# Loading the first tile in halves and reordering the first microseconds of a tuned state-space and dense block

## The chip, the cores and the metric

The kernel runs on one core of one Trainium2 chip. The metric is the device time of one execution in microseconds (us). The kernel before takes 624.6 us (median of three runs, 624.42 to 625.04). All runs quoted here are at a granted TensorE clock of 1.00 or 0.999. The profile's span is about 2 us shorter than the time.

The engines are TensorE (PE; its weight loads are PEld), VectorE (DVE), ScalarE (ACT), GpSimd (POOL) and SyncE (SP, which here only issues DMAs). A letter q after an engine's name, as in SPq, is its sequencer issuing a DMA.

## The reference

The input x is [2048, 1024]. It is normalised row by row; the result goes through a diagonal complex recurrence with two projections (branch A) and through a dense layer with the Mish function (branch B), and both are added to x.

```
xn  = (x - mean) / sqrt(var + 1e-5)                  # per row
A   = 2 * Re(C @ h),  h[t] = Lam_bar * h[t-1] + B_bar @ xn[t],   plus xn * Dskip
B   = act(xn @ w1 + b1) @ w2,   act(h) = h * tanh(softplus(h))
out = x + A + B
```

## The kernel before

The 2048 rows are worked in four blocks of 512 rows, each of four tiles of 128 rows. In each block TensorE does the first dense layer (28 column groups f, 8 matmuls each), the input projection of the recurrence, and then the second dense layer and the output projection. Everything before the first real matmul of block 0 is the head: the rows must be loaded, normalised and transposed. That is what the change is about.

Each buffer has a record of its last writer and readers, and a helper turns it into semaphore waits; so the order of the calls below is the order on each engine. `vop`, `aop` and `pop` queue an operation on VectorE, ScalarE and GpSimd.

```
    for q in range(NQ):                      # four tiles of x, 256 KB each, on SyncE's queue
        load_x(SP, 0, q)
    ...                                      # then w1 (seven ring slots of 512 KB) on the same queue

    keep_busy(76)                            # 76 filler matmuls before the transposes
    ...
    for q in range(2):                       # tiles 0 and 1: sums on VectorE
        first_sums_v(q, 0)
        first_sums_v(q, 1)
        first_var_v(q)
    first_sqrt(0)
    first_mean_a(2)                          # tile 2: sums on ScalarE
    first_sqrt(1)
    first_var_a(2)
    first_sqrt(2)
    first_apply(0)                           # xn of tile 0, VectorE
    first_transpose(0)                       # 8 transposes on TensorE into PSUM
    keep_busy(4)
    first_apply(1)
    first_transpose(1)
    keep_busy(4)
    first_copy(0, VE)                        # PSUM to SBUF
    first_copy(1, VE, 0, 4)
    first_copy(1, AC, 4, NK)
    first_mean_a(3)                          # tile 3: sums on ScalarE
    first_var_a(3)
    first_sqrt(3)
    first_apply(2)
    first_apply(3)
    NSPLIT = 6
    # [...]
    for f in range(NSPLIT):
        first_half(f, 0)                     # 8 matmuls of 256 columns: tiles 0 and 1 only
        if f == 0:
            ...                              # transpose of the parameters, copy to par
        if f in (2, 3):
            q = f
            first_transpose(q)               # tiles 2 and 3 join here
            first_copy(q, VE)
```

After f=5 the second halves of f=0 to 5 (tiles 2 and 3) follow, and from f=6 on matmuls have all 512 columns. So f=6 is where the head's effect ends for TensorE.

GpSimd works through a chain of phases that starts when VectorE has computed `thp`, which it does in program order right after the copy of tile 3:

```
    def phases(j):                           # eight times, all on GpSimd
        xs, b_xs = ph_slot(j)
        pop(... px = iot * thp[j] ...)
        pop(... py = round(px) ...)
        pop(... xs = px - py ...)
```

VectorE in block 0 evicts the dense layer's results (`hb`), multiplies the Mish results (`act<-act,hb`, "mish products"), computes statistics for block 1, and multiplies the projection by tables (`mt<-ps,tab`, two operations for each of eight j). TensorE needs the PSUM banks of the last of those products before it can go on with the second dense layer.

Of the kernel before, what the change touches and what calls it, by code (L numbers as in the profile page):

```python
# [5 lines left out]
ALU = mybir.AluOpType  # L6
# [3 lines left out]
P = 128  # L10
# [146 lines left out]
def build_kernel(nc, A_x, A_Lambda_re, A_Lambda_im, A_B_re, A_B_im, A_C_re, A_C_im,  # L157
                 A_log_dt, A_Dskip, B_w1, B_b1, B_w2, out):
    bf16, f32, i32 = DT.bfloat16, DT.float32, DT.int32
    S, D = A_x.shape[1], A_x.shape[2]  # L160
# [4 lines left out]
    NQ = TB // P  # L165
    NK = D // P
# [8 lines left out]
    PE = Queue(nc, "pe")  # L175
    VE = Queue(nc, "ve")
    AC = Queue(nc, "ac")
    PO = Queue(nc, "po")
    SP = Queue(nc, "sp")

    def sb(name, shape, dtype):
        return nc.alloc_sbuf_tensor(name, shape, dtype)
# [4 lines left out]
    b_ring = [Buf("ring%d" % i) for i in range(NRING)]  # L187
# [16 lines left out]
    b_xnT = [Buf("xnT%d" % q, parts=[Buf("xnT%d_%d" % (q, h)) for h in range(2)]) for q in range(NQ)]  # L204
# [3 lines left out]
    xx = sb("xx", [P, 2, NQ, D], bf16)  # L208
    b_xx = [[Buf("xx%d_%d" % (i, q), parts=[Buf("xx%d_%d_%d" % (i, q, h)) for h in range(2)])
             for q in range(NQ)] for i in range(2)]  # L210
# [7 lines left out]
    NST = 3 * NJ + NF  # L218
    st = sb("st", [NST, P], bf16)
    b_st = Buf("st")  # L220
    ident = sb("ident", [P, P], bf16)
    b_ident = Buf("ident")
    par = sb("par", [P, NST], f32)
    b_par = Buf("par")
    stats = sb("stats", [P, 2, 2, 6], f32)
    b_stats = [Buf("stats%d" % i) for i in range(2)]
# [21 lines left out]
    ps = nc.alloc_psum_tensor("ps", [P, 8, TB], f32)  # L248
    b_ps = [Buf("ps%d" % i) for i in range(8)]

    def ps16(i):
        return ps[:, i, :].bitcast(bf16)
# [23 lines left out]
    vop, aop, pop = VE.op, AC.op, PO.op  # L276
# [7 lines left out]
    def load_x(queue, blk, q):  # L284
        r0 = blk * TB + q * P
        i = blk % 2
        queue.dma(lambda e: e.dma_start(xx[:, i, q, :], A_x[0, r0:r0 + P, :]),  # L287
                  s_xx[i][q] if blk else s_x0[q], writes=[b_xx[i][q]])

    for q in range(NQ):  # L290
        load_x(SP, 0, q)
    for src, r0, n in ((A_log_dt, 2 * NJ, NJ), (A_Lambda_im, NJ, NJ), (A_Lambda_re, 0, NJ),
                       (B_b1, 3 * NJ, NF)):
# [42 lines left out]
    def rc(q, n):  # L336
        return rs[:, q, n:n + 1]

    def first_sums_v(q, h):
        s = q % 2  # L340
        vop(lambda e: e.bn_stats(stats[:, s, h, :], xx[:, 0, q, h * 512:(h + 1) * 512]),
            reads=[b_xx[0][q]], writes=[b_stats[s]])

    def first_var_v(q):
        s = q % 2
        vop(lambda e: e.bn_aggr(mv[:, q, :], stats[:, s, :, :]), reads=[b_stats[s]], writes=[b_mv[q]])

    def first_mean_a(q):
        aop(lambda e: e.activation(sq[:], xx[:, 0, q, :], AF.Identity, bias=kon[:, 1:2], accum_out=rc(q, 3)),  # L349
            reads=[b_xx[0][q], b_kon], writes=[b_sq, b_rs[q]])  # L350
        aop(lambda e: e.activation(mv[:, q, 0:1], rc(q, 3), AF.Copy, scale=-1.0 / D),  # L351
            reads=[b_rs[q]], writes=[b_mv[q]])

    def first_var_a(q):
        aop(lambda e: e.activation(sq[:], xx[:, 0, q, :], AF.Square, bias=mv[:, q, 0:1], accum_out=mv[:, q, 1:2]),
            reads=[b_xx[0][q], b_mv[q]], writes=[b_sq, b_mv[q]])

    def first_sqrt(q):
        scale = 1.0 if q < 2 else 1.0 / D
        aop(lambda e: e.activation(rc(q, 1), mv[:, q, 1:2], AF.Sqrt, scale=scale, bias=kon[:, 2:3]),  # L360
            reads=[b_mv[q], b_kon], writes=[b_rs1[q]])

    def first_apply(q):
        y = rc(q, 1)
        vop(lambda e: e.reciprocal(y, y), reads=[b_rs1[q]], writes=[b_rs1[q]])  # L365
        vop(lambda e: e.tensor_scalar(xn[:, q, :], xx[:, 0, q, :], mv[:, q, 0:1], y,  # L366
                                      op0=ALU.subtract if q < 2 else ALU.add, op1=ALU.mult),
            reads=[b_xx[0][q], b_mv[q], b_rs1[q]], writes=[b_xn[q]])

    def bank_T(q, k):  # L370
        if q == 1 and k >= NK // 2:
            return 5
        return 6 + q % 2

    def first_transpose(q):
        for k in range(NK):
            bank = bank_T(q, k)
            PE.mm(lambda e, k=k, bank=bank: e.transpose(ps16(bank)[:, k * P:(k + 1) * P],  # L378
                                                        xn[:, q, k * P:(k + 1) * P], ident[:]),
                  reads=[b_xn[q], b_ident], writes=[b_ps[bank]],  # L380
                  first=k == 0 or bank != bank_T(q, k - 1), last=k == NK - 1 or bank != bank_T(q, k + 1))

    def first_copy(q, queue, k0=0, k1=NK):
        dst = xnT[:, k0:k1, q * P:(q + 1) * P]
        bank = bank_T(q, k0)
        srcp = ps16(bank).rearrange("p (k t) -> p k t", k=NK)[:, k0:k1, :]
        b_dst = b_xnT[q] if k1 - k0 == NK else b_xnT[q].parts[k0 // 4]
        if queue is AC:
            aop(lambda e: e.copy(dst, srcp), reads=[b_ps[bank]], writes=[b_dst])  # L389
        else:  # L390
            vop(lambda e: e.tensor_copy(dst, srcp), reads=[b_ps[bank]], writes=[b_dst])
# [62 lines left out]

    def keep_busy(n):
        for i in range(n):
            PE.mm(lambda e: e.matmul(ps[:, 4, 0:P], lhsT=ident[:], rhs=ident[:], start=True, stop=True),
                  reads=[b_ident], writes=[b_ps[4]], first=i == 0, last=i == n - 1)

    keep_busy(76)  # L460
    aop(lambda e: e.activation(rs[:, :, 3], kon[:, 2:3].to_broadcast([P, NQ]), AF.Sqrt), reads=[b_kon], writes=b_rs)
    for q in range(2):
        first_sums_v(q, 0)
        first_sums_v(q, 1)
        first_var_v(q)
    first_sqrt(0)
    first_mean_a(2)
    first_sqrt(1)
    first_var_a(2)
    first_sqrt(2)  # L470
    first_apply(0)
    first_transpose(0)
    keep_busy(4)
    first_apply(1)
    first_transpose(1)
    keep_busy(4)
    first_copy(0, VE)
    first_copy(1, VE, 0, 4)
    first_copy(1, AC, 4, NK)
    first_mean_a(3)  # L480
    first_var_a(3)
    first_sqrt(3)
    first_apply(2)
    first_apply(3)
    NSPLIT = 6

    def first_half(f, half):
        s, fi = f // 2, f % 2
        wt = ring[:, s, :].rearrange("p (k f) -> p k f", k=NK)
        ts = slice(half * 256, half * 256 + 256)  # L490
        for k in range(NK):
            PE.mm(lambda e, k=k: e.matmul(ps[:, f, ts], lhsT=wt[:, k, fi * P:(fi + 1) * P], rhs=xnT[:, k, ts],  # L492
                                          start=k == 0, stop=k == NK - 1),
                  reads=[b_ring[s]] + b_xnT[2 * half:2 * half + 2], writes=[b_ps[f]],
                  first=half == 0 and k == 0, last=half == 1 and k == NK - 1)

    for f in range(NSPLIT):
        first_half(f, 0)
        if f == 0:
            PE.op(lambda e: e.transpose(ps16(5)[:, 0:NST], st[:, :], ident[0:NST, 0:NST]),  # L500
                  reads=[b_st, b_ident], writes=[b_ps[5]])
            vop(lambda e: e.tensor_copy(par[:, :], ps16(5)[:, 0:NST]), reads=[b_ps[5]], writes=[b_par])
        if f in (2, 3):
            q = f
            first_transpose(q)
            first_copy(q, VE)

# [123 lines left out]
    def first_tile(blk, f):  # L631
        s = n_item[0] % NRING
        fi, bank, hs = f % 2, f % 8, f % (2 * GF)
        wt = ring[:, s, :].rearrange("p (k f) -> p k f", k=NK)
        if blk == 0 and f < NSPLIT:
            first_half(f, 1)
        for k in range(0 if blk == 0 and f < NSPLIT else NK):
            PE.mm(lambda e, k=k: e.matmul(ps[:, bank, :], lhsT=wt[:, k, fi * P:(fi + 1) * P], rhs=xnT[:, k, :],  # L638
                                          start=k == 0, stop=k == NK - 1),
                  reads=[b_ring[s]] + b_xnT, writes=[b_ps[bank]], first=k == 0, last=k == NK - 1)  # L640
        if fi == 1:
            item_done()
        if f % GF == 0 and f >= 2 * GF:
            mish_mul(f // GF - 2)
        vop(lambda e: e.tensor_scalar(hb[:, hs, :], ps[:, bank, :], b1(f), None, op0=ALU.add),  # L645
            reads=[b_ps[bank], b_par], writes=[b_hbf[hs]])
        if f % GF == GF - 1:
            mish(f // GF)
# [219 lines left out]
```

## Time and profile before

| quantity | value | where |
|---|---|---|
| time, median of 3 | 624.6 us | runs |
| span | 622.4 us | page |
| TensorE's share of the chain that ended last | 98% | page, part 4 |
| first real matmul | 9.78 us | timeline |
| first weight load of f=6 | 21.28 us | timeline |
| TensorE idle after 9.78 us, as the view counts it | 0.27 us, at 93 us | waits, timeline |

The first fence is the page, its lines for busy time and for the chain. The chain is followed back from the last instruction to what released each step.

```profile
PE 616.7 (99%) x2981; PEld 287.9 (46%) x2981; DVE 464.1 (75%) x684; ACT 246.7 (40%) x162; POOL 50.2 (8%) x47
...
PE 98%; DMA 1%; DVE 1%; ACT 0%; SPq 0%; issue 0%
```

TensorE is the bottleneck, and the rest of the chain is the head. The next fence is the timeline of the head (start, duration, engine, line, operation, output<-input, shapes, count; in brackets the idle time before it and what ended it).

```profile
0.79 1.84 SPq L287 DMA_DIRECT2D xx<-in_A_x_dram  x4
...
1.41 5.65 PE L457 MATMUL ps<-ident 128*128 128x128 bf16 x76 [1.41 <-POOL kon L328]
...
2.67 5.67 SPq L316 DMA_DIRECT2D ring<-in_B_w_dram  x4
...
3.57 1.42 DVE L341 BATCH_NORM_STATS2 stats<-xx 128x6 f32<-128x512 bf16 x2 [3.57 <-DMA xx<-in_A_x_dram]
...
5.90 1.15 ACT L349 ACTIVATE sq<-xx,kon 128x1024 bf16<-128x1024 bf16 x1 [0.34 <-DMA xx<-in_A_x_dram]
...
7.28 0.28 ACT L360 ACTIVATE rs<-mv,kon 128x1 f32<-128x1 f32 x1
7.43 0.62 PE L378 MATMUL ps<-ident,xn 128*128 128x128 bf16 x8 [0.36 <-DVE xn L366]
...
7.79 0.55 DVE L366 TENSOR_SCALAR xn<-xx,mv,rs 128x1024 bf16<-128x1024 bf16 x1
...
9.78 1.03 PE L492 MATMUL ps<-xnT,ring 128*128 128x256 bf16 x8 [0.54 <-ACT xnT L389]
```

The root of tile 1 (7.28) stands behind ScalarE's mean of tile 2 (5.90), and so tile 1 is normalised only at 7.79.

The chain in order of time, from the end of the head to block 1:

```profile
21.55 37.99 PE ps L638 x176
59.54 27.63 PE ps L658 x128
87.17 3.47 PE ps L715 x16
90.63 0.00 issue
90.64 2.37 DVE mt L663 x2
93.00 0.05 issue
93.05 70.54 PE ps L715 x326
163.58 6.47 PE ps L638 x30
```

At 90.64 the chain leaves TensorE for VectorE's last `mt` product and comes back at 93.05.

### The profile page before, as it was taken

Reading aid. Unit: us, or ns where it says so; the run is one execution under the profiler, and the core shown is the slowest. Engines: PE = TensorE matmul, PEld = TensorE weight load, DVE = VectorE, ACT = ScalarE, POOL = GpSimd, SP = SyncE. Lnnn points to the kernel's source line nnn. Section 1 sums busy time; section 2 is a strip of 40 time slices with the busy share of each in tenths; the row PEclk is TensorE's granted clock in tenths of the full one; section 3 lists DMA queues with packets and bytes.
Section 4 is the critical chain, followed back from the end, with each engine's and each line's share of the span. In section 5 each row is a group of like instructions: output and inputs, shape, how many; then the busy total and the mean of one; then the engine's idle time right before and its main releaser. Section 6 shows DMA issues by size and latency. Waiting matters only on the chain.

```text
span 622.4 us, 7441 instructions
## 1 busy us (share of the span) xinstructions
PE 616.7 (99%) x2981; PEld 287.9 (46%) x2981; DVE 464.1 (75%) x684; ACT 246.7 (40%) x162; POOL 50.2 (8%) x47
## 2 busy tenths in 40 slices
PE   8999999999999999999999999999999999999998
PEld 7644444444444444444444444444444444444443
DVE  5799999999557599998147759999624856999603
ACT  6679995341069940000008992000001999000000
POOL 1999000000100000000010000000000000000000
PEclk9999999999999999999999999999999999999999
DMA  9999966750364300863055420285204531043001
GB/s 264 235 296 263 213 134 198 191 153 1 128 195 150 135 2 28 205 195 113 17 186 157 148 102 1 89 216 162 77 34 136 168 135 70 0 136 101 1 0 68
DMA packets 124188, 79.41 MB, mean 128 GB/s; under 512 B 48890, under 2 KB 106490, under 8 KB 124154
## 3 DMA queue, kind: packets, MB, share of 16 engines
q1 hardware_dynamic: 120656, 71.58, 42.5%
q10 hardware_dynamic: 2538, 4.21, 1.8%
q0 software_dynamic: 960, 3.15, 1.5%
q8 instruction: 24, 0.39, 0.3%
q14 instruction: 10, 0.08, 0.0%
HBM read 63.19 MB, written 4.19 MB: 108 GB/s over the span
## 4 chain that ended last, share of the span: by engine, by line
PE 98%; DMA 1%; DVE 1%; ACT 0%; SPq 0%; issue 0%
PE ps L715 49%; PE ps L638 29%; PE ps L658 18%; PE ps L492 2%; DMA xx<-in_A_x_dram 1%; DVE mt L663 0%; PE ps L378 0%; ACT sq L349 0%; SPq L287 0%; DVE xx L752 0%; ACT xnT L389 0%; DVE xn L366 0%; ACT mv L351 0%; ACT rs L360 0%; DVE rs L365 0%
## 5 line engine op out<-in xcount | busy, mean ns | idle before, releaser
L715 PE MATMUL ps<-ring,act 128*128 128x512 bf16 x896 | 194.2, 379 | 0.3 <-DVE mt L663 0.3
L638 PE MATMUL ps<-xnT,ring 128*128 128x512 bf16 x848 | 183.7, 379 | 0.0
L616 ACT ACTIVATE act<-hb 128x3584 bf16<-128x3584 bf16 x16 | 50.9, 3183 | 245.5 <-DVE hb L645 245.2
L715 PEld LDWEIGHTS ps<-ring,act 128*128 128x128 bf16 x896 | 87.6, 98 | 106.2 <-DVE mt L663 0.8
L638 PEld LDWEIGHTS ps<-xnT,ring 128*128 128x128 bf16 x848 | 83.0, 98 | 99.9
L645 DVE TENSOR_SCALAR hb<-ps,par 128x512 bf16<-128x512 f32 x112 | 82.8, 747 | 56.3 <-PE ps L638 54.4
L715 PE MATMUL ps<-CT,hT 128*128 128x512 bf16 x512 | 111.2, 379 | 0.0
L658 PE MATMUL ps<-xnT,BT 128*128 128x512 bf16 x512 | 111.2, 379 | 0.0
L663 DVE TENSOR_TENSOR mt<-ps,tab 128x1024 bf16<-128x1024 f32 x64 | 75.3, 1218 | 13.3 <-PE ps L658 11.8
L658 PEld LDWEIGHTS ps<-xnT,BT 128*128 128x128 bf16 x512 | 50.1, 98 | 60.4
L715 PEld LDWEIGHTS ps<-CT,hT 128*128 128x128 bf16 x512 | 50.1, 98 | 60.4
L752 DVE TENSOR_TENSOR xx<-ps,xx 128x1024 bf16<-128x1024 f32 (+1 forms) x17 | 19.5, 1159 | 70.3 <-PE ps L715 70.2
L681 DVE TENSOR_TENSOR_SCAN hT<-cs,qi,hT 128x512 bf16<-128x512 f32 x48 | 58.9, 1267 | 0.0
L618 ACT ACTIVATE act<-act 128x3584 bf16<-128x3584 bf16 x16 | 51.0, 3190 | 0.2
L617 ACT ACTIVATE act<-act 128x3584 bf16<-128x3584 bf16 x16 | 51.0, 3190 | 0.2
L686 DVE TENSOR_TENSOR mt<-hT,tab 128x1024 bf16<-128x1024 bf16 x64 | 41.4, 688 | 1.1
L623 DVE TENSOR_TENSOR act<-act,hb 128x3584 bf16<-128x3584 bf16 x16 | 32.9, 2058 | 1.3 <-ACT act L618 1.3
L287 POOL DMA_DIRECT2D xx<-in_A_x_dram x12 | 6.7, 559 | 254.0 <-DVE xx L752 249.9
L592 ACT ACTIVATE ct<-CT,cs 128x512 f32<-128x512 bf16 x16 | 11.5, 718 | 28.8 <-DVE CT L594 24.5
L617 ACT ACT_TABLE_LOAD x16 | 20.5, 1283 | 0.3
L618 ACT ACT_TABLE_LOAD x16 | 20.5, 1283 | 0.3
L681 DVE TENSOR_TENSOR_SCAN hT<-cs,hT 128x512 bf16<-128x512 f32 x16 | 18.7, 1207 | 0.0
(78 smaller groups left out, 277.2 us busy)
## 6 DMA issues: line engine op xcount, KB each, us to landing
ring<-in_B_w_dram SPq DMA_DIRECT2D x112, 512.0 KB, 3.7
out_dram<-xx ACTq DMA_DIRECT2D x15, 256.0 KB, 2.0
xx<-in_A_x_dram POOLq DMA_DIRECT2D x12, 256.0 KB, 4.1
xx<-in_A_x_dram SPq DMA_DIRECT2D x4, 256.0 KB, 3.6
dsk<-in_A_Dskip_dram SPq DMA_DIRECT2D x1, 256.0 KB, 6.7
out_dram<-xx ACTq DMA_DIRECT2D x2, 128.0 KB, 1.7
xnT<-xn SPq DMA_TRANSPOSE x12, 4.4
BT<-in_A_B_re_dram SPq DMA_TRANSPOSE x8, 5.7
```

Source lines behind the costliest of these rows:

```text
L616: aop(lambda e: e.activation(a, hs, AF.Exp), reads=[b_hb[g % 2]], writes=[b_act[g]])
L617: aop(lambda e: e.activation(a, a, AF.Ln, bias=1.0), reads=[b_act[g]], writes=[b_act[g]])
L618: aop(lambda e: e.activation(a, a, AF.Tanh), reads=[b_act[g]], writes=[b_act[g]])
L623: vop(lambda e: e.tensor_tensor(a, a, hs, op=ALU.mult), reads=[b_act[g], b_hb[g % 2]], writes=[b_act[g]])
L638: PE.mm(lambda e, k=k: e.matmul(ps[:, bank, :], lhsT=wt[:, k, fi * P:(fi + 1) * P], rhs=xnT[:, k, :], start=k == 0, stop=k == NK - 1), rea ...
L645: vop(lambda e: e.tensor_scalar(hb[:, hs, :], ps[:, bank, :], b1(f), None, op0=ALU.add), reads=[b_ps[bank], b_par], writes=[b_hbf[hs]])
L658: PE.mm(lambda e, j=j, ci=ci, k=k, bank=bank: e.matmul(ps[:, bank + ci, :], lhsT=BT[:, ci, j, k, :], rhs=xnT[:, k, :], start=k == 0, stop= ...
L663: vop(lambda e, s=s, u=u, j=j: e.tensor_tensor(mt[:, s, :, :], u, tab[:, s, j, :].unsqueeze(1).to_broadcast([P, 2, TB]), op=ALU.mult), rea ...
L681: vop(lambda e, ci=ci, init=init: e.tensor_tensor_scan(out=hT[:, ci, j, :], data0=cj("r", j).to_broadcast([P, TB]), data1=hT[:, ci, j, :], ...
L686: vop(lambda e, s=s: e.tensor_tensor(mt[:, s, :, :], hT[:, :, j, :], tab[:, s, j, :].unsqueeze(1).to_broadcast([P, 2, TB]), op=ALU.mult), ...
L715: PE.mm(lambda e: e.matmul(ps[:, u, :], lhsT=lhsT, rhs=rhs, start=st_, stop=last), reads=reads, writes=[b_ps[u]], first=st_, last=last)
L752: vop(lambda e: e.tensor_tensor(xr, src, xr, op=ALU.add), reads=b_src + [b_x], writes=[b_x])
```

## The change

Intent: start the statistics earlier (half of tile 0 suffices), take tile 2's sums off ScalarE so that they no longer delay tile 1, and let the first four matmuls start once the lower halves of the transposed tiles are copied. The diff, cut to its core:

```
-    for q in range(NQ):
+    for h in range(2):
+        SP.dma(lambda e, h=h: e.dma_start(xx[:, 0, 0, h * 512:(h + 1) * 512], A_x[0, 0:P, h * 512:(h + 1) * 512]),
+               DmaSem(nc, "d_x00_%d" % h), writes=[b_xx[0][0].parts[h]])
+    for q in range(1, NQ):
         load_x(SP, 0, q)
# [...]  bank_T: upper halves of tiles 0 and 1 go to banks 4 and 5; fillers go to bank 3
     keep_busy(76)
# [...]
+    PE.op(... transpose of the parameters into bank 2 ...)
     for q in range(2):
         first_sums_v(q, 0)
         first_sums_v(q, 1)
         first_var_v(q)
-    first_sqrt(0)
-    first_mean_a(2)
-    first_sqrt(1)
-    first_var_a(2)
-    first_sqrt(2)
+        first_sqrt(q)
     first_apply(0)
     first_transpose(0)
     keep_busy(4)
     first_apply(1)
     first_transpose(1)
-    keep_busy(4)
-    first_copy(0, VE)
+    first_copy(0, VE, 0, 4)
     first_copy(1, VE, 0, 4)
+    first_mean_a(3)
+    first_copy(0, AC, 4, NK)
     first_copy(1, AC, 4, NK)
-    first_mean_a(3)
     first_var_a(3)
     first_sqrt(3)
+    vop(... copy of the parameters to par ...)
+    for h in range(2):
+        first_sums_v(2, h)
+    first_var_v(2)
+    first_sqrt(2)
     first_apply(2)
     first_apply(3)
# [...]  first_half: matmuls k=0..3 wait for the lower half of xnT only
     for f in range(NSPLIT):
         first_half(f, 0)
-        if f == 0:
-            ...                              # transpose and copy of the parameters
-        if f in (2, 3):
-            q = f
+        if f in (2, 4):
+            q = 1 + f // 2
             first_transpose(q)
             first_copy(q, VE)
```

More of the change, by code (lines that the diff above doesn't have):

```diff
@@ L341, in first_sums_v @@
         vop(lambda e: e.bn_stats(stats[:, s, h, :], xx[:, 0, q, h * 512:(h + 1) * 512]),
-            reads=[b_xx[0][q]], writes=[b_stats[s]])
+            reads=[b_xx[0][q].parts[h]], writes=[b_stats[s]])
     def first_var_v(q):
@@ L358, in first_sqrt @@
     def first_sqrt(q):
-        scale = 1.0 if q < 2 else 1.0 / D
+        scale = 1.0 if q < 3 else 1.0 / D
         aop(lambda e: e.activation(rc(q, 1), mv[:, q, 1:2], AF.Sqrt, scale=scale, bias=kon[:, 2:3]),
@@ L366, in first_apply @@
         vop(lambda e: e.tensor_scalar(xn[:, q, :], xx[:, 0, q, :], mv[:, q, 0:1], y,
-                                      op0=ALU.subtract if q < 2 else ALU.add, op1=ALU.mult),
+                                      op0=ALU.subtract if q < 3 else ALU.add, op1=ALU.mult),
             reads=[b_xx[0][q], b_mv[q], b_rs1[q]], writes=[b_xn[q]])
     def bank_T(q, k):
-        if q == 1 and k >= NK // 2:
-            return 5
+        if q < 2 and k >= NK // 2:
+            return 4 + q
         return 6 + q % 2
@@ L456, in keep_busy @@
         for i in range(n):
-            PE.mm(lambda e: e.matmul(ps[:, 4, 0:P], lhsT=ident[:], rhs=ident[:], start=True, stop=True),
-                  reads=[b_ident], writes=[b_ps[4]], first=i == 0, last=i == n - 1)
+            PE.mm(lambda e: e.matmul(ps[:, 3, 0:P], lhsT=ident[:], rhs=ident[:], start=True, stop=True),
+                  reads=[b_ident], writes=[b_ps[3]], first=i == 0, last=i == n - 1)
     keep_busy(76)
     aop(lambda e: e.activation(rs[:, :, 3], kon[:, 2:3].to_broadcast([P, NQ]), AF.Sqrt), reads=[b_kon], writes=b_rs)
+    PE.op(lambda e: e.transpose(ps16(2)[:, 0:NST], st[:, :], ident[0:NST, 0:NST]),
+          reads=[b_st, b_ident], writes=[b_ps[2]])
     for q in range(2):
@@ L475, in build_kernel @@
     first_transpose(1)
-    keep_busy(4)
-    first_copy(0, VE)
+    first_copy(0, VE, 0, 4)
     first_copy(1, VE, 0, 4)
+    first_mean_a(3)
+    first_copy(0, AC, 4, NK)
     first_copy(1, AC, 4, NK)
-    first_mean_a(3)
     first_var_a(3)
     first_sqrt(3)
+    vop(lambda e: e.tensor_copy(par[:, :], ps16(2)[:, 0:NST]), reads=[b_ps[2]], writes=[b_par])
+    for h in range(2):
+        first_sums_v(2, h)
+    first_var_v(2)
+    first_sqrt(2)
     first_apply(2)
@@ L493, in first_half @@
                                           start=k == 0, stop=k == NK - 1),
-                  reads=[b_ring[s]] + b_xnT[2 * half:2 * half + 2], writes=[b_ps[f]],
+                  reads=[b_ring[s]] + [b.parts[k // 4] for b in b_xnT[2 * half:2 * half + 2]], writes=[b_ps[f]],
                   first=half == 0 and k == 0, last=half == 1 and k == NK - 1)
@@ L498, in build_kernel @@
         first_half(f, 0)
-        if f == 0:
-            PE.op(lambda e: e.transpose(ps16(5)[:, 0:NST], st[:, :], ident[0:NST, 0:NST]),
-                  reads=[b_st, b_ident], writes=[b_ps[5]])
-            vop(lambda e: e.tensor_copy(par[:, :], ps16(5)[:, 0:NST]), reads=[b_ps[5]], writes=[b_par])
-        if f in (2, 3):
-            q = f
+        if f in (2, 4):
+            q = 1 + f // 2
             first_transpose(q)
```

## The prediction

> **What bounds it now.** TensorE. The chain of waits gives it 98% of the 622.4 us span; from 9.78 us, the first real matmul, to the end it idles only 0.27 us (waits of TensorE: at 93.0 us, for VectorE's mt products of block 0). The change touches only what precedes about 17 us, so it can win at most idle head, and some 7 of the 9.78 us are DMA and statistics that no reordering removes. A win over 2% (12.5 us) is not there.
>
> **The head before (chain, timeline).** x tile 0 lands at 3.57, tile 1 before 5.15, tile 2 at 5.88, tile 3 at about 6.8 (issue 2.2 plus the longest landing, 4.6). VectorE: sums of tiles 0 and 1 to 6.55, apply(0) 6.83. ScalarE puts the mean of tile 2 (5.90 to 7.37) before the root of tile 1 (7.28), so apply(1) starts at 7.79, its transposes 8.40; copies end 9.64, first matmul 9.78; f=1 starts at 10.95, after a 0.13 us parameter transpose.
>
> **What changes, costed.**
> 1. Half loads: [...] First half at 3.2 to 3.3, second (issued 0.46 later) at 3.6 to 3.8, inside the first bn_stats (0.71). Stats start 0.3 to 0.4 earlier; tile 1's aggregate at about 6.2. Cost: a fifth issue of 0.46, so tile 3 lands later, about 7.0.
> 2. Tile 2's mean leaves ScalarE: the root of tile 1 follows its aggregate at once; apply(1) ends near 7.65, not 8.34.
> 3. Half copies: both lower halves by about 8.55, the first four matmuls near 8.7. But ScalarE does the mean of tile 3 first: from its landing (7.0) 1.38 us to the next operation (trace: 5.90 to 7.28), then two 0.5 to 0.6 us copies, to about 9.45. Matmuls k=4 to 7 start near 9.6, f=1 near 10.1, against 10.95. [...] So the gain is set by ScalarE's mean of tile 3: TensorE should show a new wait of 0.4 to 0.9 us inside f=0.
> 4. Tile 2's sums on VectorE (1.6 us) follow the copies; its root queues behind ScalarE's variance of tile 3 (1.3). xn of tile 2 is ready near 12.0, just when TensorE finishes f=2: 0 to 0.3 us of stall. Tile 3's transposes move one f later, so its copy (0.69) has only f=5 (0.9) as cover: 0 to 0.1.
> 5. The parameter transpose moved into the idle head: 0.13 (counted in 3).
>
> **Sum.** 0.85 minus about 0.15: 0.7 us. It should survive block 0: VectorE is busy without a gap from 28.5 to 93.0, but its last idle, at 28.50, is a wait for a matmul, so that stretch moves with TensorE.
>
> **Prediction: 623.9 us, 8 in 10 between 623.3 and 624.5. Faster by over 2%: 0.005; within 2%: 0.99; slower by over 2%: 0.005.**
>
> **Right if:** first bn_stats near 3.25; apply(1) near 7.1; first real matmul near 8.7, then a wait for ScalarE's xnT copy; f=1 near 10.1; f=6 (first 512-column matmuls) about 0.7 earlier than 21.55; the rest of the chain shifted alike.
>
> **Wrong if:** tile 3 lands by 6.6 (gain 1.1) or after 7.4 (0.4); 1 KB rows make the halves as slow as the whole; tile 2's transposes wait over 0.5 us; or VectorE's stretch to 93 us, with its irregular long operations while GpSimd works, lengthens and gives the gain back as a longer wait there.

The landings of 3.2 to 3.3 and 3.6 to 3.8, the 0.3 to 0.4 us and what follows from them were not worked out from a trace; the runs below measure them. The forecast's sum came to 0.7 us (624.6 less 0.7 is 623.9): 0.85 us is step 3's f=1, at 10.1 instead of 10.95, counted from a landing of tile 3 at 7.0, and about 0.15 us are the stalls of step 4.

## The result

The changed kernel takes 624.28 us (median of 5, 623.55 to 624.46) against 624.42 us (median of 5) for the kernel before in the same rounds. The ratio is 0.9993, with a 95% interval of 0.9979 to 1.0006. Ratios are the mean time of one kernel's runs over that of the other's of the same rounds, so not quite the ratio of the medians quoted. Executions over 1.5% slower than the fastest of the same kernel are left out of the means. Repeated, the changed kernel took 624.16 us (ratio 0.9991, 0.9979 to 1.0004). The predicted 623.9 us, with 623.3 to 624.5, holds; but the profile does not show what the prediction said would happen.

The timeline of the changed kernel's head:

```profile
0.79 0.88 SPq L291 DMA_DIRECT2D xx<-in_A_x_dram  x2
...
1.41 5.71 PE L460 MATMUL ps<-ident 128*128 128x128 bf16 x76 [1.41 <-POOL kon L331]
...
3.15 6.04 SPq L319 DMA_DIRECT2D ring<-in_B_w_dram  x4
3.16 1.50 DVE L344 BATCH_NORM_STATS2 stats<-xx 128x6 f32<-128x512 bf16 x2 [3.16 <-DMA xx<-in_A_x_dram]
...
7.15 0.55 DVE L369 TENSOR_SCALAR xn<-xx,mv,rs 128x1024 bf16<-128x1024 bf16 x1
...
7.74 1.15 ACT L352 ACTIVATE sq<-xx,kon 128x1024 bf16<-128x1024 bf16 x1 [0.98 <-DMA xx<-in_A_x_dram]
...
9.58 3.02 PE L498 MATMUL ps<-xnT,ring 128*128 128x256 bf16 x24 [1.10 <-DMA ring<-in_B_w_dram]
```

The statistics did start 0.41 us earlier, and tile 1 was normalised 0.64 us earlier. But ring 0, the first weights, was issued 0.48 us later and took 6.4 instead of 5.9 us, so the first matmul, whose part of xnT was copied by 8.71, waits for its weights (TensorE idles 1.10 us before it), and starts at 9.58. Tile 3 lands at 7.7 instead of 6.8, so ScalarE's mean of it starts at 7.74. The waits of the weight loads show what follows (who waited for whom: us in total, times, longest):

```profile
PEld ps L498 <- DMA ring<-in_B_w_dram: 1.3, 1, 1.3
PEld ps L381 <- DVE xn L369: 0.3, 1, 0.3
PEld ps L498 <- ACT xnT L392: 0.3, 1, 0.3
PEld ps L717 <- DVE mt L665: 0.3, 1, 0.3
PEld ps L498 <- DVE xnT L394: 0.2, 1, 0.2
```

The upper copies (ACT xnT), tile 2 (DVE xn) and tile 3's copy (DVE xnT) each add a small wait. (The line with `mt` is a weight load that waits beside running matmuls, 0.8 us in the kernel before; the list of the matmuls' own waits has no `mt` any more.) At f=6 nothing of the gain is left: the chain in order of time shows its 512-column matmuls starting at 21.68, where the kernel before had 21.55.

```profile
21.68 37.99 PE ps L640 x176
59.66 27.63 PE ps L660 x128
87.29 75.97 PE ps L717 x352
163.26 6.91 PE ps L640 x32
```

The third line is 0.44 us shorter, 75.97 us instead of 76.41 (from 87.17 to 163.58), because the visit to VectorE at 90 us is gone; less what the head lost, that is the difference of the two spans (622.4 and 622.1). TensorE no longer waits for the last `mt` product. So the head lost 0.13 us, and a stage 70 us later, that no line of the diff names, won 0.44 us.

### The profile page after: what moved, and what is told of

Read it like the earlier page. It is cut to its first block, busy times and chain, and to the rows that moved or that the text cites. A ratio compares the mean times of both kernels' runs of the same rounds, so it can differ in the third digit from the quotient of the medians.

```text
span 622.1 us, 7433 instructions
## 1 busy us (share of the span) xinstructions
PE 616.5 (99%) x2977; PEld 287.5 (46%) x2977; DVE 465.6 (75%) x687; ACT 244.5 (39%) x158; POOL 49.9 (8%) x47
## 3 DMA queue, kind: packets, MB, share of 16 engines
q0 software_dynamic: 960, 3.15, 1.6%
## 4 chain that ended last, share of the span: by engine, by line
PE 97%; DMA 1%; ACT 1%; SPq 0%; DVE 0%; issue 0%
PE ps L717 49%; PE ps L640 29%; PE ps L660 18%; PE ps L498 1%; DMA xx<-in_A_x_dram 1%; ACT sq L352 0%; ACT sq L358 0%; PE ps L381 0%; ACT xnT L392 0%; SPq L287 0%; SPq L291 0%; DVE xx L754 0%; DVE xn L369 0%; ACT rs L363 0%; ACT mv L354 0%
```

## The experiments

Three pieces of the profile add up to TensorE's whole course and are steadier than the run times, which scatter by a microsecond (in e_best4's profile with the end of the last output DMA): the start of the first real matmul; from there to the first weight load of f=6 ("filling in"); and from there to the start of the last addition of VectorE ("body"). All runs, in us:

| run | first matmul | filling in | body | median time | ratio (95%) |
|---|---|---|---|---|---|
| before, first profile | 9.78 | 11.50 | 598.18 | 624.6 | |
| r_before | 9.64 | 11.49 | 598.25 | 624.27 | 0.9995 (0.9982 to 1.0007) |
| e_half_only | 10.20 | 11.49 | 598.21 | 624.82 | 0.9997 (0.9983 to 1.001) |
| e_pool_late | 9.70 | 11.49 | 597.79 | 624.01 | 0.9997 (0.9983 to 1.0011) |
| changed, first profile | 9.58 | 11.83 | 597.73 | 624.28 | 0.9993 (0.9979 to 1.0006) |
| r_after | 9.85 | 11.46 | 597.74 | 624.16 | 0.9991 (0.9979 to 1.0004) |
| e_whole | 9.19 | 11.46 | 597.73 | 623.33 | 0.9983 (0.997 to 0.9995) |
| e_t3 | 9.91 | 11.93 | 598.70 | 624.44 | 1.0002 (0.999 to 1.0015) |
| e_fill56 | 9.76 | 11.38 | 597.73 | 623.86 | 0.9998 (0.9985 to 1.0011) |
| e_best1 | 9.14 | 11.45 | 597.74 | 623.34 | 0.9993 (0.998 to 1.0005) |
| e_best2 | 9.24 | 11.45 | 597.74 | 623.26 | 0.9985 (0.9972 to 0.9997) |
| e_best3 | 9.24 | 11.58 | 597.83 | 623.74 | 0.999 (0.9978 to 1.0002) |
| e_best4 | 9.34 | 11.33 | 597.82 | 624.53 | 0.9994 (0.9982 to 1.0007) |
| e_best5 | 9.31 | 11.58 | 598.23 | 623.8 | 0.9988 (0.9976 to 1.0) |

The effects at stake are 0.1 to 0.7 us, the intervals are about 0.8 us to either side. So a single ratio rarely decides; the pieces of the profile do, where they repeat. The body is one number plus the stall near 93 us. From start to start of the matmuls the stall is 0.43, 0.50, 0.46 and 0.48 us in before, r_before, e_half_only and e_best5, 0.96 us in e_t3 and at most 0.08 us in the others; the body less its stall is 597.73 to 597.75 us in all fourteen profiles.

Theory 1 was that the half loads delay all later loads and so take away the head's gain. Theory 2 was that the body's gain comes from GpSimd's chain: tile 3's transposes moved from behind f=3 to behind f=4, so VectorE computes `thp` later (which it does in program order right after the copy of tile 3), so GpSimd's chain runs some 0.8 us later against the other two (its first multiply starts 5.4 us before f=6's weight load in the kernel before, at 15.84, and 4.7 before in the changed one, at 16.75), and meets other VectorE operations. The rival to both was scatter from run to run.

### r_before and r_after: both kernels again

No edit.

> The kernel before once more, unchanged: the noise floor, and a second profile. If late landings are caused by the half loads (theory), tile 3 lands again near 6.8 us and the first weight ring near 8.6, f=6 starts near 21.4; if the landings only scatter from run to run (rival), they differ by some 0.5 us or more from the first profile. VectorE's gapless stretch to the last mt product of block 0 was 64.5 us with a TensorE stall of 0.27 after it; if its length is chance, it differs by tenths here. Ratio to before 1.0000, within 0.0005.

> The changed kernel once more: a second profile. Theory (half loads delay later loads): tile 3 lands again near 7.7, ring 0 near 9.5, f=6 starts near 21.5, so the head wins nothing, and the ratio is 0.9993 to 1.0000, decided by the stall near 93 us. Rival (scatter): tile 3 near 6.8 to 7.2, ring 0 below 9.2, f=6 earlier than 21.2 and ratio 0.9985 to 0.9992.

The kernel before: tile 3 landed at 6.5, ring 0 at 8.3, body 598.25, with the stall. The changed kernel: tile 3 at 7.3, ring 0 at 9.05, body 597.74, no stall. The bodies repeat to 0.07 and 0.01 us while they differ by 0.5, so the body's gain is not chance. The landings lie between the two expectations: ring 0 at 9.05 is below the rival's 9.2, tile 3 at 7.3 is between 7.2 and 7.7, and f=6 is later than the rival's 21.2. The head is again no better: f=6's weight load at 21.13 before and at 21.31 changed. But the reason in this profile is another one. TensorE's timeline of r_after:

```profile
1.42 6.69 PE L460 MATMUL ps<-ident 128*128 128x128 bf16 x76 [1.42 <-POOL kon L331]
8.04 0.20 PE L465 MATMUL ps<-ident,st 52*128 52x52 bf16 x1
8.17 0.62 PE L381 MATMUL ps<-ident,xn 128*128 128x128 bf16 x8
```

The same 76 fillers took 6.69 us instead of 5.71, and the transposes of tile 0 queued behind them until 8.17, although xn of tile 0 was ready at 6.84. The reason can be read from the matmuls that TensorE starts per microsecond (the stretches view; its columns are the stretch, us with work, TensorE's busy time and matmuls, granted clock, DMA share, GB/s): 12 to 13 while its matmuls are slow, 19 to 22 later. In the first profile of the kernel before the fast rate is there in the stretch from 4 us on; in r_after, in the one from 6 us on.

```profile
3.00:4.00 1.00, 1.00 (x12) 1.00 1.20 327
4.00:5.00 1.00, 1.00 (x12) 1.00 1.04 304
5.00:6.00 1.00, 1.00 (x13) 1.00 0.75 215
6.00:7.00 1.00, 1.00 (x19) 1.00 0.90 271
```

The moment differs between runs: in the eight profiles with 76 fillers the gap from one filler's start to the next falls from 107 to 56 ns between 2.6 and 5.2 us after the first, and the fillers take 5.65 to 6.90 us. What sets the moment is not shown: the granted clock reads 1.00 in the slow stretches as well. A filler count that was harmless before the change holds up a head that got ready earlier.

### e_whole: the changed kernel with tile 0 loaded whole

```
-    for h in range(2):
-        SP.dma(... half h of tile 0 ...)
-    for q in range(1, NQ):
+    for q in range(NQ):
         load_x(SP, 0, q)
```

> The changed kernel with tile 0 loaded whole again (one issue fewer, rows of 2 KB). Theory: first bn_stats back at 3.57 (0.4 later), but tile 3 lands at 6.8 and ring 0 at 8.6, so ScalarE's mean of tile 3 starts near 7.1, the first matmul starts near 9.1, k=4 near 9.7, and f=6 at 21.0 to 21.2: 0.3 to 0.5 us faster than the changed kernel. Rival (landings scatter, the half loads are a gain): f=6 at 21.5 or later, not faster than the changed kernel.

The statistics start at 3.51 instead of 3.16. Tile 3 lands at 6.6 and ring 0 at 8.67; the first matmul starts at 9.19, and the matmuls' list has no wait for weights left (that of the weight loads still puts 0.5 us down to ring 0, but it had landed by then); f=6's weight load is at 20.65, 0.76 and 0.66 us before the two profiles of the changed kernel:

```profile
20.65 2.37 PEld L637 LDWEIGHTS ps<-xnT,ring 128*128 128x128 bf16 x12
```

The time is 623.33 us, ratio 0.9983, and its interval (0.997 to 0.9995) excludes 1. So one part of the change was worth undoing. That does not make the predicted gain of the head right: this head is 0.48 to 0.63 us earlier at f=6 than the two profiles of the kernel before, not 0.7, and about 0.5 us of the 1.0 to 1.1 us by which the span is shorter are the body's. TensorE's wait list of this run names VectorE's last copies before the first matmul (0.4 us), which again stood behind the fillers (6.03 us, to 7.45; xn of tile 0 was ready at 7.32).

### e_half_only: the kernel before with the half loads alone

The edit is the half load of the diff above and the sums of tile 0 waiting for their half.

> The kernel before with the half loads alone. Theory: first bn_stats at 3.15, but tile 3 at 7.7 and ring 0 at 9.5; ScalarE's copy still ends near 9.3 to 9.6, so the first matmul starts at 9.6 to 9.7 and the time is that of before, within 0.2 us (ratio 0.9997 to 1.0002). Rival (half loads are the gain): first matmul at 9.4 or earlier with ring 0 in time, ratio 0.9994 or lower.

The statistics start at 3.08, but the first matmul at 10.20, later than predicted by either theory. Tile 3 landed at 6.4, against theory 1, so ScalarE was not late here; ring 0 landed at 9.25. The culprit is again the fillers, 6.90 us in this run: tile 0's transposes started at 8.15 though xn was ready at 6.96. The half loads alone gave nothing (624.82 us, ratio 0.9997), but with long fillers in its profile the run says little about the head that they would give otherwise.

Over all runs, the five profiles with both halves on SyncE's queue and the seven with a whole load compare as follows (means; each landing is the time of the issue plus the time to landing, which the view rounds to 0.1 us):

| | halves on SyncE | whole |
|---|---|---|
| first bn_stats starts | 3.04 (2.92 to 3.16) | 3.53 (3.39 to 3.62) |
| tile 3 lands | 7.23 (6.4 to 8.3) | 6.64 (6.0 to 7.5) |
| ring 0 issued | 3.15 | 2.67 |
| ring 0 lands | 9.49 (9.05 to 9.85) | 8.54 (8.27 to 9.27) |

So the halves bring 0.49 us at the front and cost 0.95 us at the weights: 0.48 of it is the fifth issue on the queue, 0.47 a longer time to landing (6.34 against 5.87 us). The first repeats to 0.01 us; the second, like tile 3's delay, is a difference of means between groups that overlap (5.9 to 6.7 and 5.6 to 6.6 us). Why it takes longer to land was not separated further.

### e_pool_late: the kernel before, with GpSimd's chain 0.8 us later

```
     turns()
+    pop(lambda e: e.tensor_scalar(px[:, 0:240], iot[:, 0:240], cj("thp", 0), None, op0=ALU.mult),
+        reads=[b_iot, b_cs["thp"]], writes=[b_px])
     for j in range(NJ):
         phases(j)
```

> The kernel before, with one extra 240-column GpSimd multiply (about 0.75 us) ahead of its phase chain, so that the chain runs about 0.8 us later against TensorE and VectorE, as it does in the changed kernel; nothing else. Theory (the changed kernel's gain is a shift of GpSimd's chain, which changes how VectorE's operations are held up): the head stays (f=6 weight load near 21.2 to 21.3), the time from it to the last mt product of block 0 falls from 69.4 to 68.9 us, TensorE's 0.27 us stall at 93 us goes, the two mish products (4.64 us before, 3.98 after) fall to about 4.0, ratio about 0.9993. Rival (the order or the number of VectorE's own operations is the cause): mish products stay 4.64, stall stays, ratio 1.0000.

It came as theory 2 said. The extra multiply took 0.90 us (0.75 expected), and the chain's first multiply of 512 columns started at 16.75 instead of 15.84. This extra work on an engine that is busy 8% of the span made TensorE's course shorter: the body falls from 598.18 to 597.79, and the two mish products from 4.64 to 3.98 us in all. TensorE waits for no `mt` product any more, and its chain has no visit to VectorE:

```profile
87.08 76.03 PE ps L717 x352
```

The medians differ by 0.32 us (624.01 and 624.33 in these rounds); one run of 624.73 leaves the ratio of means at 0.9997.

The timelines around the first mish product show a piece of how it comes about. The kernel before:

```profile
40.90 2.26 POOL L520 TENSOR_SCALAR py<-px 128x512 f32<-128x512 f32 x1
41.28 2.43 DVE L623 TENSOR_TENSOR act<-act,hb 128x3584 bf16<-128x3584 bf16 x1
43.25 1.59 POOL L522 TENSOR_TENSOR ph_h<-px,py 128x512 f32<-128x512 f32 x1
```

The same with GpSimd's chain shifted (e_pool_late):

```profile
41.08 2.01 DVE L625 TENSOR_TENSOR act<-act,hb 128x3584 bf16<-128x3584 bf16 x1
41.59 3.31 POOL L520 TENSOR_SCALAR py<-px 128x512 f32<-128x512 f32 x1
```

And the changed kernel:

```profile
41.21 2.01 DVE L625 TENSOR_TENSOR act<-act,hb 128x3584 bf16<-128x3584 bf16 x1
41.71 3.31 POOL L522 TENSOR_SCALAR py<-px 128x512 f32<-128x512 f32 x1
```

In these three timelines whoever comes later takes longer. In the kernel before GpSimd's `py` was under way when the mish product started, and the product took 2.43 us (`py` itself had come after another operation of VectorE, `xx<-xx,mt` from 40.67 to 41.36, and took 2.26). In the other two the product started first and took 2.01, and `py` took 3.31 us instead of the 1.94 it takes undisturbed; but GpSimd, busy 8% of the span, is far from critical. The product did not wait for the whole of `py`: with 1.88 us of `py` still to run, it lost only 0.42 us. Why the one waits for the other, no trace or run here shows. Smaller operations of VectorE show the waiting better (kernel before):

```profile
58.34 1.94 POOL L520 TENSOR_SCALAR py<-px 128x512 f32<-128x512 f32 x1
58.44 0.53 DVE L408 TENSOR_SCALAR rv<-rv 128x4 int32<-128x4 int32 x1
59.21 0.16 DVE L413 TENSOR_TENSOR rv<-rv 128x4 f32<-128x4 f32 x1
60.36 1.27 POOL L522 TENSOR_TENSOR ph_a<-px,py 128x512 f32<-128x512 f32 x1
60.39 1.26 DVE L415 TENSOR_SCALAR rv<-rv 128x4 f32<-128x4 f32 x1
```

The operation of VectorE at 58.44 ends 0.63 us after this `py` starts (it takes 0.53 us, the next one of its kind, at 59.00, 0.17); the two-input operation at 59.21 runs beside `py` in its usual 0.16 us. The one at 60.39, 4 columns wide, ends with the subtraction `ph_a`: it takes 1.26 us, where the same line takes 0.17 at 59.60. In the fourteen profiles 145 two-input operations on `rv` or `cs` start within a `py`: the 14 that start in its first 0.16 us end 0.62 to 0.63 us after its start, and the other 131 take no more than 0.2 us. One-input operations are not so clear: some on `cs` end only with a `py` (two from 29.96 to 30.51 us in the changed kernel, where `py` ends at 30.47), and what decides it stays open.

It matters because VectorE has no gap from 28.50 us to the last `mt` product at 93 us in the kernel before, and the sum of its delays decides whether TensorE gets its banks in time. The mish products are a mark of the shift and not the whole of it. From the eviction at 28.50 us (28.62 in the changed kernel, in both 7.2 us after f=6's weight load) to the end of the last `mt` product are 64.49 us before and 64.03 changed. The mish products give 0.66 us of that, the small operations on the parameters (`cs`, with their waits) 1.29; the four `mt<-xn,dsk` (3.43 instead of 2.71 us), the `xx<-xx,mt` (0.37 more) and the small operations of block 1's statistics (`rv`, 0.38 more) take 1.47 back. It is only the balance that fell.

### e_t3: the changed kernel with tile 3's transposes after f=3

```
-        if f in (2, 4):
-            q = 1 + f // 2
+        if f in (2, 3):
+            q = f
```

> The changed kernel with tile 3's transposes back after f=3. Theory of the head: the wait for tile 3's copy before the second halves (0.15 to 0.2 us) goes, f=6 weight load near 21.15 to 21.2. But the copy and so VectorE's small operations and GpSimd's chain start 0.9 us earlier again, so by the theory of the shifted chain the mish products go back to 4.64 and the 0.27 us stall at 93 us returns: ratio 0.9995 to 1.0000, not better than the changed kernel's. Rival: stall stays away, ratio 0.9987 to 0.9990.

The stall came back, as theory 2 said (0.8 us, and mish products 4.47), ratio 1.0002. But this profile is of the slowest of its runs (625.45 us) and has two accidents: tile 3 landed at 8.3, and VectorE waited 0.9 us for a late load of block 1's rows, which is in its body of 598.70. So it supports theory 2 and does not measure it; e_best5 below is the cleaner test. The 0.2 us wait for tile 3's copy was not in TensorE's list any more, but the filling in was 11.93 because tile 3 and the weights were late.

### e_fill56: the changed kernel with 56 fillers

```
-    keep_busy(76)
+    keep_busy(56)
```

> The changed kernel with 56 instead of 76 filler matmuls. Theory: the 76 fillers last 5.7 to 6.9 us by the moment at which the matmuls get fast, and their end (7.1 to 8.1) now holds up the first transposes, which xn of tile 0 allows at 6.9; with 56 they end by 5.9 to 7.1 and the transposes start at 6.9 to 7.2 in each profile. The first matmul is then set by ring 0 (9.05 to 9.55) and ScalarE's copies: f=6 weight load 20.9 to 21.3, ratio 0.9985 to 0.9991. Rival (fillers needed to keep matmuls fast): the eight transposes of tile 0, 0.62 us, take 1.0 or more, and the time is not better than the changed kernel's.

Inconclusive for the time (median 623.86, two runs above 625, ratio 0.9998). The transposes stayed at 0.62 us, so fewer fillers did no harm here. They started at 7.58, later than expected, and this time not for the fillers (5.68 us, to 7.09) but for xn of tile 0, because VectorE had waited 0.44 us for tile 1 and normalises tile 0 only after tile 1's sums. The first matmul waited for ring 0 until 9.76 (0.9 us). So with halves on SyncE's queue the weights were the limit once the fillers were out of the way (one profile).

### e_best1: whole load, 56 fillers, ScalarE reordered

```
+    first_copy(0, AC, 4, NK)
+    first_copy(1, AC, 4, NK)
     first_mean_a(3)
-    first_copy(0, AC, 4, NK)
-    first_copy(1, AC, 4, NK)
-    first_var_a(3)
-    first_sqrt(3)
     ...                                     # par, sums of tile 2 on VectorE
     first_sqrt(2)
+    first_var_a(3)
+    first_sqrt(3)
```

This and the two lines of e_whole and e_fill56.

> The changed kernel with the whole load of tile 0, 56 fillers, ScalarE's two copies before its mean of tile 3, and the root of tile 2 before the variance of tile 3. Transposes of tile 0 at 7.3 to 7.4, first matmul near 9.0 without a wait inside f=0, no wait for tile 2: f=6 weight load near 20.4 to 20.5, no stall at 93 us, span 621.0, ratio 0.9978 to 0.9981. If instead ring 0 lands after 9.0 the first matmul starts with it.

Transposes at 7.47, first matmul at 9.14, f=6's weight load at 20.59, span 621.2: close to what was expected, but only 0.06 us better than e_whole's profile. The median is the same, 623.34 us; a run of 625.4 and one of 624.4 leave the ratio at 0.9993.

### e_best2: e_best1 with tile 0 in halves, the second issued by ScalarE

```
     for h in range(2):
-        SP.dma(... half h of tile 0 ...)
+        (SP, AC)[h].dma(... half h of tile 0 ...)
```

> As e_best1 (56 fillers, ScalarE's copies before its mean, root of tile 2 first), but with tile 0 in halves, the second half issued by ScalarE instead of SyncE, so that SyncE issues nothing more than before. If the late landings of the changed kernel come from its fifth issue on SyncE, tile 3 lands at 6.5 to 6.9 and ring 0 at 8.3 to 8.7 with the stats starting near 3.1: first matmul 8.6 to 8.8, f=6 weight load 20.2 to 20.3, 0.3 us before e_best1. Rival (rows of 1 KB load the DMA engines): ring 0 lands after 8.9 and f=6 is not before 20.5.

A miss, and an instructive one (f=6's weight load at 20.69, not 20.2 to 20.3): the first half landed no earlier than a whole tile. Both halves were issued at 0.79 and 0.80 and took 2.8 to 3.0 us, and the statistics started at 3.63. So the two halves, issued side by side by two engines, landed within 0.2 us of each other, as late as a whole tile (2.6 to 2.8 us in the seven profiles with a whole load). Put one behind the other on SyncE's queue, the first half landed after 2.1 to 2.3 us (five profiles). Ring 0 landed at 8.7 here and at 9.2 in e_best3, so without the fifth issue most of its delay was gone; two profiles are too few to show whether the shorter rows have a share in the rest. The time, 623.26 us and ratio 0.9985, is that of e_whole.

### e_best3, e_best4, e_best5: tile 3's transposes after f=3 again

e_best4 is e_best1 with the edits of e_t3 and of e_pool_late; e_best5 is the same without GpSimd's extra multiply; e_best3 is e_best2 with both.

> e_best2 with tile 3's transposes after f=3 and the extra GpSimd multiply that keeps its chain late. f=6 weight load 20.0 to 20.1, no stall at 93 us, mish products 4.0: span 620.6 to 620.8, the fastest of all.

> e_best1 with tile 3's transposes after f=3 and the extra GpSimd multiply. The 0.19 us wait for tile 3's copy goes: f=6 weight load near 20.4; GpSimd's chain stays late, mish products 3.98, no stall at 93 us: span near 621.0.

> e_best4 without the extra GpSimd multiply: head as in e_best4 (f=6 near 20.4), but GpSimd's chain is 0.8 us earlier against TensorE. Theory of the shifted chain: mish products 4.64, last mt product 69.4 us after f=6's weight load, TensorE stalls about 0.3 near 92, span 0.4 us longer than e_best4 (621.3 to 621.4). Rival: as e_best4.

The pair e_best4 and e_best5 differs in nothing but GpSimd's extra multiply. The body is 597.82 with it and 598.23 without it, the mish products 3.98 and 4.65 us, and only e_best5 has the stall in TensorE's waits:

```profile
PE ps L714 <- DVE mt L662: 0.3, 1, 0.3
```

That is theory 2 once more, in a kernel with another head. e_best5 differs from e_best1, too, in one edit alone, the place of tile 3's transposes, and e_best1 has a body of 597.74 and no stall. The wait for tile 3's copy, which these were to win back, was won at most in e_best4: filling in took 11.58, 11.33 and 11.58 us, against 11.45 in e_best1 and e_best2. f=6's weight load came at 20.82, 20.67 and 20.89, where 20.0 to 20.1 and twice 20.4 were expected. The run times do not show the pair's 0.4 us: the medians are even the other way round (624.53 for e_best4, with runs from 623.38 to 625.37, and 623.8 for e_best5); only the fastest runs, 623.38 and 623.76, are in the order of the bodies. In e_best4's profile, 3.2 us pass between the end of VectorE's last addition (618.49 + 0.69) and the end of the span (622.4); in the profile of the kernel before it is 2.25 us (622.4 less 619.46 and 0.69). So at least in that run the scatter is in the last output's DMA.

None of the three was the fastest of all, as had been expected of e_best3. The fastest versions are e_whole, e_best1 and e_best2, at medians of 623.3 us, and they cannot be told apart. e_whole is the simplest: the change without its half loads.

## Why the prediction was right or wrong

The number was right and the sum behind it was not. It said: 0.85 us less in the head, 0.15 us of new stalls, and a body that merely moves along. Measured were a head that is 0.13 to 0.18 us later at f=6 (21.41 and 21.31 against 21.28 and 21.13), and a body that is 0.45 us shorter in the first pair of profiles and 0.51 in the second. Two errors of opposite sign left a median 0.1 to 0.3 us shorter (624.28 us against 624.42 in the same rounds and 624.6 in the first three runs), less than half of the 0.7 us forecast. That the result fell inside the range is luck. The range also went up to 624.5, so that even the kernel before, at 624.42 in the same rounds, lies inside it.

- **Bound and size.** Right: TensorE, 98% of the chain, and nothing over 2% to win.
- **Step 1, half loads.** Right that the statistics start near 3.2 (3.16 and 2.95), a mean gain of 0.49 us instead of 0.3 to 0.4 (to landing the first half took 2.1 to 2.3 us, a whole tile 2.6 to 2.8). Wrong at "tile 3 lands later, about 7.0": it was 7.7 and 7.3 (6.4 to 8.3 over the five profiles with halves). The step that failed most is what it left out: the fifth issue also pushes the first weights back (issued at 3.15 instead of 2.67). Ring 0 landed at 8.57 before, invisible because nothing waited for it, and it became the limit when it moved to 9.55 and its users became ready earlier. The prediction had listed the loads of x and not that of the weights behind them.
- **Step 2, tile 1's root.** Right: it follows its aggregate, and apply(1) ended at 7.70 (7.65 predicted).
- **Step 3, half copies.** Wrong: the first matmul came at 9.58 and 9.85, not 8.7, although the lower halves were copied by 8.71 in the first profile, about as predicted (8.55). There ring 0 held it, and in the second profile the fillers did, through the transposes. The wait inside f=0 for ScalarE's copy is there but 0.3 us, not 0.4 to 0.9, because the first four matmuls were late themselves. That the mean of tile 3 sets the gain holds only second: e_best1, which moves it, and e_whole, which doesn't, are 0.06 us apart.
- **The fillers.** Not in the prediction at all. In the one profile that it had, they ended at 7.06, in time; they take 5.65 to 6.90 us from run to run.
- **Steps 4 and 5.** Right in size, or nearly: weight loads waited 0.3 us for tile 2 (0 to 0.3 predicted) and 0.2 us for tile 3's copy (0 to 0.1).
- **"It should survive block 0."** Wrong, in the good direction. The stretch of VectorE did move with TensorE, but it did not keep its length (64.03 instead of 64.49 us). The last point of the list of doubts named it, "its irregular long operations while GpSimd works", and expected a loss from it. The irregular operations overlap GpSimd's (the first mish product took 2.43 us with `py` under way and 2.01 where it started first), and moving tile 3's transposes behind f=4 shifted GpSimd's chain. e_pool_late has the body's gain without the change, and e_best5 loses it against e_best1 by that move alone.

What stays open: why ring 0 takes 0.47 us longer to land behind the halves (rows of 1 KB or a later place among the other loads were not tested apart), and what makes single runs of every kernel a microsecond slower than their neighbours. In e_t3's profile it was partly a late load of block 1's rows, in e_best4's the last output; more was not looked into.

## What to carry to other kernels

Before splitting a load to get its first half sooner, list everything behind it on the same queue with its landing time and its slack: here the first weights landed 0.95 us later on average, a slack spent without any trace in the profile before. Filler work with a fixed count is a wait in disguise once its user becomes ready earlier, and one profile shows one of its lengths (5.65 to 6.90 us here). Where VectorE runs without a gap and GpSimd works beside it, look for what a shift of GpSimd's chain does to VectorE's length: here a shift of 0.8 to 1.0 us against TensorE went with a body 0.4 to 0.5 us shorter (changed kernel, e_pool_late, e_best4); compare the stretch after the edited one as well, count a stall of TensorE from start to start, and don't credit the edit with what only the alignment did.
